# Retention and gated FFN on one core: x of pair 1 copied out by two engines and multiplied in chunks of 128 tokens, one v load and a few steps at other places

## The chip, the core and the metric

One core of a Trainium2 chip runs the whole program in one launch. TensorE (PE) multiplies, VectorE (DVE) and ScalarE (ACT) read its results out of PSUM, GpSimd (POOL) adds and multiplies in SBUF and issues the converting loads, SyncE (SP) issues stores and DMA transposes. The metric is device time in microseconds (us); lower is better.

## The reference, cut to what matters

```
B, H, S, D = 4, 8, 768, 64
gamma = 1.0 - 2.0 ** (-5.0 - np.arange(H))
for t in range(S):
    state = gamma * state + outer(k[:, :, t], v[:, :, t])
    y[:, :, t] = (q[:, :, t] @ state) / sqrt(D)
x = y.transpose(0, 2, 1, 3).reshape(3072, 512)
gate = sigmoid(x @ w_gate)             # 512 x 1536
out = (gate * (x @ w_val)) @ w_out     # 1536 x 512
```

A decaying linear attention over 4 batches and 8 heads gives x of 3072 tokens by 512; a sigmoid-gated FFN with 1536 hidden columns follows. Inputs and output are fp32 in HBM; the kernel multiplies in bf16.

## The kernel before, in words

The recurrence is done by chunks of 128 tokens. A *tile* t (0 to 5) is one chunk of each of the four batches: 512 columns of the FFN. It is made of two *pairs*: pair P holds chunk P//2 of batches 0 and 1 (P even) or 2 and 3 (P odd), and c (0, 1) is the batch in it. For each pair and c: q and k are transposed to `qkT` (on PE, lines 193 to 210, or by DMA, line 219), `scores` (line 238) multiplies them, `mask` (line 243, DVE) applies the decay and gives `st` in bf16, `inter` (line 253) multiplies q with the carried state, `intra` (line 258) adds `st` times v, and `y_out` (lines 261 to 273) writes 128 columns of `xT`, the FFN's input. `state` (line 280, PE), `state_sum` (lines 287 and 290, DVE) and `state_out` (line 295, ACT) carry the state on. The FFN of a tile goes by blocks of 128 hidden columns: gate and value products on PE (lines 305 and 309, four along d_model), the sigmoid on ACT (line 329), gate times value on DVE (line 332). Tile 1 takes blocks two by two over half of its columns (`up_half`, `half_sigmoid`, `half_finish`). Later tiles use a seven-product scheme, whose sums of weights and of hidden columns are prepared on POOL and DVE (lines 361, 456 and 474).

`mm` (line 303) issues a product either whole (128 weight columns, line 305) or as two halves of 64 weight columns (line 309); a step whose name is written in capitals is issued whole.

Two things set the order. First, straight code up to line 622: loads, the attention of pairs 0 and 1, and the first FFN block of tile 0, which starts on columns 0 to 255 (pair 0) and goes on with columns 256 to 511 (pair 1). Then `ORDER`, one string a tile, is read from left to right, and each word issues one step: `mk10` is mask number 10 (pair 2, c 1, half 0), `in5` and `ia5` are `inter` and `intra` of pair 2, c 1, `yo5` is its `y_out`, `vm11` the value block 11 and `mu11` its finish, `sg` a sigmoid, `tp7` and `te7` the PE transpose of q of pair 3 and its copy on ACT, `ag2` and `ag6` gate blocks of tile 1 over its first 256 columns, `sc6` scores of pair 3, `sm5` the state products of pair 5, `zs` and `zo` its sum and copy, `dp`, `dc`, `da`, `ds` products, copies, adds and stores of the second FFN product, `hs` and `hg` sums of hidden columns on DVE and POOL, `wp` and `aw` sums of weights on POOL. A `+` or `-` behind a word takes it for the next or the previous tile. Every engine works through its own part of this list in order, and waits are on counters of the other engines.

PSUM has eight banks; one holds the state products and seven are handed out by a table, `PLACES["ff"]`, in order of use. So a step that takes a bank waits until the bank's last reader is done. `PLACES["st"]` does the same for the masked scores.

Loads of k, q and v that convert to bf16 go through POOL's queue (line 96). Pair 5 is the second half of tile 2's k, q and v. Eight counters serve these loads in turn: the ninth load's issue waits until the first has landed.

Of the kernel before, what the change touches and what calls it, by code (L numbers as in the profile page):

```python
# [17 lines left out]
def kernel(  # L18
# [14 lines left out]
    C = 128  # L33
# [23 lines left out]
        "gs": "01234501234503215034203502345102354130524301453201540321453034035412031524",  # L57
        "maskd": "01",
        "ff": (
            "012345601230465102346523105246310542631405314056321602341562034163412045632516523560132601562306"  # L60
            "251062562015020324512065630653102651604250142343624015405400652016203541034046326504510416035253"
            "245132541351025162405034123406520512341234160532120605410531324"
        ),
        "qkT": "010231230123",
        "kt": "0101100101",
        "st": "012345670123456702134675120346752104637563245710",
        "xT": "010101",
        "hT": "010101",
        "scr": "010101101001101010010101010101",
# [12 lines left out]
    def held_in(P, n):  # L82
        held = {"k": kn, "q": qn, "v": vn}[n]
        t, j = divmod(P, 2)
        if (n, t) not in lands:
            lands[n, t] = place(ld, [C, 4 * H, D], BF16, tag=n, name=n + "n")
        for i in range(2):
            held[2 * t + i] = lands[n, t][:, i * 2 * H:(i + 1) * 2 * H, :]
        return held[P]

    def load(P, *what, pairs=1):
        t, j = divmod(P, 2)
        for n in what:
            held_in(P, n)
            x = {"k": k, "q": q, "v": v}[n]
            nc.gpsimd.dma_start(out=lands[n, t][:, j * 2 * H:(j + pairs) * 2 * H, :],  # L96
                                in_=x[2 * j:2 * (j + pairs), :, t * C:(t + 1) * C, :].rearrange("b h s d -> s (b h) d"))
# [85 lines left out]
    qkT, kt, sc, st, y, zz, za, xT = {}, {}, {}, {}, {}, {}, {}, {}  # L183

    def bank(shape, dt=F32):
        return place(pf, shape, dt, tag="ff", name="ff", padded_shape=[128, 2 * NP, C] if dt == BF16 else None)
# [62 lines left out]
    def inter(P, c):  # L249
        y[P, c] = bank([128, NP, C])  # L250
        if P > 1:
            for p in range(NP):
                mm(y[P, c][:, p, :], zbd[P % 2][:, c, p, :], qkT[P][:, 1, c, p, :], start=(p == 0), stop=False)

    def intra(P, c):
        for p in range(NP):
            for i in range(2):
                nc.tensor.matmul(y[P, c][i * D:(i + 1) * D, p, :], heads(vn[P], c)[:, 2 * p + i, :],  # L258
                                 st[P, c, i][:, p, :], start=(P < 2 and p == 0), stop=True, skip_group_check=True)

    def y_out(P, c, eng="a"):
        t = P // 2
        if t not in xT:
            xT[t] = place(at, [128, NP, 512], BF16, tag="xT", name="xT")
        col = (P % 2 * 2 + c) * C
        o = xT[t][:, :, col:col + C]
        if eng == "av":
            nc.scalar.copy(o[:, :NP // 2], y[P, c][:, :NP // 2])
            nc.vector.tensor_copy(o[:, NP // 2:], y[P, c][:, NP // 2:])
        elif t == 0:  # L270
            (nc.scalar.copy if eng == "a" else nc.vector.tensor_copy)(o, y[P, c])  # L271
        else:
            nc.vector.tensor_tensor(o, y[P, c], taby0, op=ALU.mult)  # L273
# [29 lines left out]
    def mm(o, left, right, **kw):  # L303
        if whole[0]:
            nc.tensor.matmul(o, left, right, skip_group_check=True, **kw)  # L305
            return
        for i in range(2):
            half = slice(i * D, (i + 1) * D)
            nc.tensor.matmul(o[half], left[:, half], right, skip_group_check=True, **kw)  # L309
# [8 lines left out]
    def up(t, n1, which, lo=0, hi=512):  # L318
        if (t, n1, which) not in us:
            us[t, n1, which] = bank([128, 512])  # L320
        w = (wg, wv)[which]
        for kk in range(KT):
            mm(us[t, n1, which][:, lo:hi], w[:, kk, n1 * 128:(n1 + 1) * 128], xT[t][:, kk, lo:hi],
               start=(kk == 0), stop=(kk == KT - 1))

    def up_sigmoid(t, n1, lo=0, hi=512):
        if (t, n1) not in gated:
            gated[t, n1] = place(ffn, [128, 512], F32, tag="gs", name="gs")
        nc.scalar.activation(gated[t, n1][:, lo:hi], us[t, n1, 0][:, lo:hi], AX.Sigmoid)
# [231 lines left out]
    def hold(P):  # L561
        nc.gpsimd.tensor_copy(kept[:, :2], qkT[P][:, :, 1, NP - 1, C - 1])

    def hold_for_sums(t):
        nc.gpsimd.tensor_copy(kept[:, 2:3], hs[t][:, 2, NFF // 2 - 1, :1])


    def y_step(P, c, eng="a"):
        inter(P, c)
        intra(P, c)  # L570
        y_out(P, c, eng)
# [26 lines left out]
    nc.scalar.preload_act_table(AX.Sigmoid)  # L598
    up(0, 0, 0, 0, 256)
    up(0, 0, 1, 0, 256)  # L600
    y_step(1, 0, "v")
    y_step(1, 1, "a")
    up_sigmoid(0, 0, 0, 256)
    up_finish(0, 0, 0, 256)
    us.clear()
    gated.pop((0, 0))
    for which in range(2):
        up(0, 0, which, 256, 512)
    up_sigmoid(0, 0, 256, 512)
    up_finish(0, 0, 256, 512)  # L610
    for s in range(3, NFF // 2 - 1):
# [7 lines left out]
    for s in range(4):  # L619
        load_out(s)  # L620
    load(4, "k", "q", "v")
    load(5, "k", "q", "v")

    STEPS = {
        "gm": lambda t, n: up(t, n, 0),
# [38 lines left out]
        "lk": lambda t, P: load(P, "k", pairs=2),  # L664
        "lq": lambda t, P: load(P, "q", pairs=2),
        "lv": lambda t, P: load(P, "v", pairs=2),
        "ho": lambda t, P: hold(P),
        "hi": lambda t, n: hold_for_sums(t),
        "xk": lambda t, P: xbar(P, 0),
# [128 lines left out]
```

## Time and profile before

| what | value |
|---|---|
| time before, median of 3 runs | 224.1 us (224.1, 226.42, 215.31) |
| the profiled execution's own time | 215.9 us |
| its span, first to last instruction | 214.2 us |
| clock granted to TensorE in it | 1.000 |
| PE busy | 204.6 us of the span, 96% |
| DVE, ACT, POOL busy | 189.2, 147.5, 139.5 us |
| HBM read, written | 28.31 MB, 6.29 MB |

Times in the profile count from the start of the span. In a timeline a row is: start, duration, engine, line, operation, output <- inputs, shape (partitions*weight columns for a PE row), count, and in brackets the idle time before it and what ended it. A PE row of several matmuls runs until the last result is out; the next row may begin before, since matmuls are pipelined. So the pace of a stream is read from start to start. "PEld" is the loading of weights.

### The profile page before, as it was taken

How to read it: one execution, taken by the hardware profiler on the slowest of the kernel's cores; microseconds unless marked ns; L12 is line 12 of the kernel's file. 1: busy time of each engine (PE TensorE's matmuls, PEld its weight loads, DVE VectorE, ACT ScalarE, POOL GpSimd, SP SyncE). 2: the span in 40 equal slices, each digit the busy share in tenths (PEclk: the TensorE clock that was granted, in tenths of full speed). 3: DMA queues.
4: the chain of work that ended last, by engine and by line, in shares of the span. 5: the costliest groups of instructions: out<-in, count | busy, mean ns of one | idle time of the engine just before them, and what ended most of it. 6: DMA issues, size and time to landing. Idle time of an engine off the chain costs nothing.

```text
span 214.2 us, 7187 instructions
## 1 busy us (share of the span) xinstructions
PE 204.6 (96%) x2938; PEld 177.3 (83%) x2938; DVE 189.2 (88%) x406; ACT 147.5 (69%) x396; POOL 139.5 (65%) x145
## 2 busy tenths in 40 slices
PE   6778999999999999999999999999999999999994
PEld 6555555778888998899988889998899988888883
DVE  6587979989999999979999899999999999968971
ACT  6384466543994389786869798787768969577731
POOL 8977784679999946699764279875618537024500
PEclk9999999999999999999999999999999999999999
DMA  9999999999995999969995129998121000023305
GB/s 125 143 170 194 195 173 165 183 199 159 159 132 33 98 156 143 204 126 157 170 227 115 49 99 163 159 105 127 49 101 52 3 0 3 0 50 70 75 25 183
DMA packets 103922, 25.38 MB, mean 118 GB/s; under 512 B 93904, under 2 KB 101072, under 8 KB 103888
## 3 DMA queue, kind: packets, MB, share of 16 engines
q0 software_dynamic: 81104, 13.90, 84.6%
q1 hardware_dynamic: 22640, 10.88, 28.6%
q8 instruction: 23, 0.38, 0.7%
q10 hardware_dynamic: 144, 0.13, 0.2%
q14 instruction: 11, 0.09, 0.1%
HBM read 28.31 MB, written 6.29 MB: 162 GB/s over the span
## 4 chain that ended last, share of the span: by engine, by line
PE 76%; DMA 14%; POOL 4%; DVE 3%; issue 1%; ACT 0%; ACTq 0%; DVEq 0%; POOLq 0%
PE ff L305 41%; PE ff L309 29%; DMA qn<-in_q_dram 6%; DMA wg<-in_moe_w_gate_dram 4%; DMA vn<-in_v_dram 4%; PE ff L238 2%; PE ff L258 2%; DVE scr L414 1%; POOL kn L96 1%; PE z L280 1%; DVE gs L435 1%; DVE xT L273 1%; POOL vn L96 1%; POOL qn L96 1%; POOL kn L104 1%
## 5 line engine op out<-in xcount | busy, mean ns | idle before, releaser
L420 POOL TENSOR_TENSOR hT<-gs,scr 128x512 bf16<-128x512 f32 x17 | 22.1, 1302 | 21.4 <-ACT gs L440 9.0
L430 ACT COPY gs<-ff 128x256 f32<-128x256 f32 x72 | 25.6, 377 | 11.1 <-PE ff L305 5.7
L409 ACT COPY scr<-ff 128x256 f32<-128x256 f32 x72 | 25.2, 375 | 6.5 <-PE ff L309 3.6
L414 DVE TENSOR_TENSOR scr<-scr,ff 128x512 f32<-128x512 f32 (+1 forms) x48 | 25.6, 547 | 3.5 <-ACT scr L409 1.3
L435 DVE TENSOR_TENSOR gs<-gs,ff 128x512 f32<-128x512 f32 (+1 forms) x48 | 25.8, 548 | 3.2 <-PE ff L305 2.0
L510 ACT COPY ob<-ff 128x256 f32<-128x256 f32 x48 | 17.7, 375 | 15.2 <-PE ff L305 8.9
L243 DVE TENSOR_TENSOR st<-ff,maskd 128x512 bf16<-128x512 f32 x40 | 25.7, 682 | 0.9 <-PE ff L238 0.9
L440 ACT ACTIVATE gs<-gs 128x512 f32<-128x512 f32 (+1 forms) x48 | 24.7, 530 | 2.3 <-DVE gs L435 2.2
L309 PE MATMUL ff<-xT,wg 128*64 128x256 bf16 (+1 forms) x268 | 24.2, 308 | 0.0
L309 PEld LDWEIGHTS <-wg 128*64 128x64 bf16 x356 | 19.4, 110 | 4.1 <-issue 0.4
L423 POOL TENSOR_TENSOR hT<-gs,scr 128x256 bf16<-128x256 f32 x16 | 11.9, 747 | 15.9 <-ACT gs L440 12.0
L309 PE MATMUL ff<-xT,wv 128*64 128x256 bf16 (+1 forms) x220 | 21.5, 311 | 0.0
L305 PEld LDWEIGHTS <-hT 128*128 128x128 bf16 x198 | 19.2, 98 | 2.7 <-issue 0.2
L305 PE MATMUL ff<-wo,hT 128*128 128x256 bf16 x156 | 21.0, 273 | 0.0
L309 PEld LDWEIGHTS <-wv 128*64 128x64 bf16 x312 | 17.2, 110 | 4.2 <-issue 0.3
L305 PEld LDWEIGHTS <-wv 128*128 128x128 bf16 x184 | 17.7, 98 | 2.4
L305 PEld LDWEIGHTS <-wg 128*128 128x128 bf16 x162 | 15.7, 98 | 3.8 <-issue 1.1
L309 PE MATMUL ff<-xs,ws 128*64 128x256 bf16 x208 | 18.7, 273 | 0.0
L305 PE MATMUL ff<-xT,wv 128*128 128x256 bf16 (+1 forms) x134 | 18.5, 276 | 0.0
L231 ACT ACTIVATE kt<-kn,tabk 128x128 bf16<-128x128 bf16 x48 | 18.3, 405 | 0.1
L309 PEld LDWEIGHTS <-ws 128*64 128x64 bf16 x308 | 17.2, 110 | 0.3
L305 PE MATMUL ff<-xT,wg 128*128 128x256 bf16 x110 | 15.4, 272 | 1.6 <-ACT xT L271 1.6
(118 smaller groups left out, 526.8 us busy)
## 6 DMA issues: line engine op xcount, KB each, us to landing
out_dram<-ob SPq DMA_DIRECT2D x18, 256.0 KB, 3.3
vn<-in_v_dram POOLq DMA_DIRECT2D x6, 256.0 KB, 12.4
wo<-in_moe_w_out_dram POOLq DMA_DIRECT2D x4, 384.0 KB, 14.2
kn<-in_k_dram POOLq DMA_DIRECT2D x3, 512.0 KB, 7.8
qn<-in_q_dram POOLq DMA_DIRECT2D x3, 512.0 KB, 10.0
vn<-in_v_dram POOLq DMA_DIRECT2D x3, 512.0 KB, 11.6
out_dram<-ob SPq DMA_DIRECT2D x11, 128.0 KB, 2.2
kn<-in_k_dram POOLq DMA_DIRECT2D x5, 256.0 KB, 13.4
```

The costliest lines, as they stand in the source:

```text
L231: nc.scalar.activation(to[:, :, h, :], x[:, :, h, :], AX.Copy, scale=tabk[:, 0, h:h + 1])
L243: nc.vector.tensor_tensor(st[P, c, i], sc[P, c][i], (mask0 if P < 2 else maskd)[:, i], op=ALU.mult)
L305: nc.tensor.matmul(o, left, right, skip_group_check=True, **kw)
L309: nc.tensor.matmul(o[half], left[:, half], right, skip_group_check=True, **kw)
L409: nc.scalar.copy(vals[t, g][:, {1: 0, 5: 2, 3: 1}[n]], m[False][:, 256:] if n == 1 else m[True][:, :256])
L414: nc.vector.tensor_tensor(o, o, x, op=ALU.add)
L420: eng.tensor_tensor(h[:, 2 * g], s, vals[t, g][:, 0:2].rearrange("p two n -> p (two n)"), op=ALU.mult)
L423: eng.tensor_tensor(h[:, 2 * g + 1, 256:], s[:, 256:], vals[t, g][:, 2], op=ALU.mult)
L430: nc.scalar.copy(o, pairs[t, g, 0][x][:, :256] if x else pairs[t, g, 0][x][:, 256:])
L435: nc.vector.tensor_tensor(o, o, pairs[t, g, 0][False][:, cols], op=ALU.add)
L440: nc.scalar.activation(o, x, AX.Sigmoid)
L510: nc.scalar.copy(o, fast[t, i][x][:, :256] if x else fast[t, i][x][:, 256:])
```

## The change

1. **Prelude, pair 1.** `y_step(1, 0)` and `y_step(1, 1)` each split their copy into `xT`: ACT takes the first half of the rows p (lines 268), DVE the second (line 269). Before, DVE did the whole of c 0 and ACT the whole of c 1. The first FFN block on columns 256 to 511, a gate and a value product of four matmuls of 256 columns each, becomes gate and value on columns 256 to 383 and then on 384 to 511: 16 matmuls of 128 columns in place of 8.
2. **v of pair 5** is loaded by a new step `lw5` behind `hg6-` in tile 1's string, not with k and q of pair 5 at line 622.
3. **Tile 1's string, start.** All four masks of pair 2 come first, then `in5 in4 ia5 ia4 yo5 yo4`, and then `vm11`, `mu10` and `mu11`; `in4` is issued in two halves; the gate block `ag2` stands ahead of `tp7`.
4. **Small moves.** Farther on in tile 1, `dc11-` and `dc15-` (ACT) stand ahead of two scalings of k, and `hs7-` (DVE) ahead of `bm4`. In tile 2, `sm6` stands behind `gp57`, not ahead of `vp47`.
5. `PLACES["ff"]` and `PLACES["st"]` are numbered anew from there on.

```
-    y_step(1, 0, "v")
-    y_step(1, 1, "a")
+    y_step(1, 0, "av")
+    y_step(1, 1, "av")
...
-    for which in range(2):
-        up(0, 0, which, 256, 512)
+    for lo in (256, 384):
+        for which in range(2):
+            up(0, 0, which, lo, lo + C)
...
-    load(5, "k", "q", "v")
+    load(5, "k", "q")
...
+        "lw": lambda t, P: load(P, "v"),
...
-        "zo0- wp1 gm7- wp4 gm8- tp5- vm8- mu4- sg7- sg8- te5- gm11- sc4- sc5- gm10- sg10- mu6- mu8- mk10- mk8-  "
-        "mk11- wp8 vm10- mu10- wp2 in5 ia5 vm11- IN4 mk9- ia4 yo5 tp6 yo4 aw13 sg11- te6 mu11- tp7 te7 dd5 dd15  "
+        "zo0- wp1 gm7- wp4 gm8- tp5- vm8- mu4- sg7- sg8- te5- gm11- sc4- sc5- gm10- sg10- mu6- mu8- mk10- mk11-  "
+        "mk8- mk9- wp8 vm10- wp2 in5 in4 ia5 ia4 yo5 yo4 vm11- mu10- tp6 aw13 sg11- te6 mu11- ag2 tp7 te7 dd5  "
```

Three places of the built program show what moves. In these rows a number before the `x` of a shape is partitions, and what an instruction waits for stands in brackets: `PE_49` and `Activation_49` are the counters of PE and ACT, `DMASW1_49` one of the loads' counters.

DVE in the prelude, around the copies of x of pair 1, before:

```order
L243 TENSOR_TENSOR st<-ff,mask_123 128x512 [waits PE_49] x4
L271 CAST xT<-ff 128x4x128 [waits PE_49]
L332 TENSOR_TENSOR hT<-gs,ff 128x256 [waits Activation_49]
L332 TENSOR_TENSOR hT<-gs,ff 128x256 [waits PE_49,Activation_49]
L361 TENSOR_TENSOR ws<-wv 128x256 [waits DMASW1_49]
```

and the same engine and place now:

```order
L243 TENSOR_TENSOR st<-ff,mask_123 128x512 [waits PE_49] x4
L269 CAST xT<-ff 128x2x128 [waits Activation_49] x2
L332 TENSOR_TENSOR hT<-gs,ff 128x256 [waits Activation_49]
L332 TENSOR_TENSOR hT<-gs,ff 128x256 [waits PE_49,Activation_49]
L361 TENSOR_TENSOR ws<-wv 128x256 [waits DMASW1_49]
```

One copy of 512 elements has become two of 256, and these wait for ACT, where the one waited for PE.

DVE at the start of tile 1's string, as one piece of the difference (L243 the masks of pair 2, L332 the finishes `mu`, L273 `yo5` and `yo4`):

```order
 L332 TENSOR_TENSOR hT<-gs,ff 128x512 x3
-L243 TENSOR_TENSOR st<-ff,maskd 128x512 x3
-L332 TENSOR_TENSOR hT<-gs,ff 128x512
-L243 TENSOR_TENSOR st<-ff,maskd 128x512
-L273 TENSOR_TENSOR xT<-ff,taby_138 128x4x128 x2
-L332 TENSOR_TENSOR hT<-gs,ff 128x512
+L243 TENSOR_TENSOR st<-ff,maskd 128x512 x4
+L273 TENSOR_TENSOR xT<-ff,taby_138 128x4x128 x2
+L332 TENSOR_TENSOR hT<-gs,ff 128x512 x2
 L361 TENSOR_TENSOR ws<-ws,wg 128x256
```

The fourth mask and both outputs of x have moved ahead of a finish (`mu10`).

POOL, as two pieces of the difference: where the loads of tile 2 end and the sums of weights begin, and 14 instructions later, behind `hg6` (L474):

```order
 L96 DMA kn<-in_k_dram 128x16x64
 L96 DMA qn<-in_q_dram 128x16x64
-L96 DMA vn<-in_v_dram 128x16x64
 L361 TENSOR_TENSOR ws<-wv 128x256
 L456 TENSOR_TENSOR wt<-wo 128x512
```

Here the issue is gone; the second piece, behind the sum `hg6`, has it:

```order
 L361 TENSOR_TENSOR wg<-wg 128x2x128
 L474 TENSOR_TENSOR hT<-hT 128x2x256
+L96 DMA vn<-in_v_dram 128x16x64
 L456 TENSOR_TENSOR wt<-wo,scr 128x512
 L456 TENSOR_TENSOR scr<-wo 128x512
```

The load of v has moved past 14 sums that POOL makes.

More of the change, by code (lines that the diff above doesn't have):

```diff
@@ L59 @@
         "ff": (
-            "012345601230465102346523105246310542631405314056321602341562034163412045632516523560132601562306"
-            "251062562015020324512065630653102651604250142343624015405400652016203541034046326504510416035253"
-            "245132541351025162405034123406520512341234160532120605410531324"
+            "012345601230465102346523105246310542631405314056321632045631205430541256301643610634201432461036"
+            "142361461324313015421364603640231642635143251050615324534533641326130452305356016435423526304140"
+            "154201452042314261534305210536413421052105263401213634523402015"
         ),
@@ L65 @@
         "kt": "0101100101",
-        "st": "012345670123456702134675120346752104637563245710",
+        "st": "012345670123456701234675210346751204637563145720",
         "xT": "010101",
```

12 rows, old and new, of the table ORDER are left out of this document.

## Prediction

> **What bounds the kernel now.** I read the page first: the slices of the span and the chain that ended last. The granted clock is 1.000 (table above), so no part of the sum hangs on it.
>
> ```profile
> PE   6778999999999999999999999999999999999994
> ...
> PE 76%; DMA 14%; POOL 4%; DVE 3%; issue 1%; ACT 0%; ACTq 0%; DVEq 0%; POOLq 0%
> ```
>
> From the fifth of 40 slices on (21 us) PE is at nine tenths or more, and three quarters of the chain are PE. The change removes no matmul, so it can only win or lose in the few places where PE waits. Then I read the timeline of each engine at the places that the diff touches. The end of the prelude on PE (intra of pair 1, gate, value, the first block of the string):
>
> ```profile
> 16.30 0.64 PE L258 MATMUL ff<-st,vn 128*64 128x128 bf16 x16
> 17.61 0.60 PE L305 MATMUL ff<-xT,wg 128*128 128x256 bf16 x4 [0.68 <-ACT xT L271]
> 18.05 0.60 PE L305 MATMUL ff<-xT,wv 128*128 128x256 bf16 x4
> ```
>
> PE stands for 0.68 us there, for the two copies of x, which run side by side on two engines:
>
> ```profile
> 16.75 0.69 DVE L271 CAST xT<-ff 128x512 bf16<-128x512 f32 x1 [0.98 <-PE ff L258]
> 16.98 0.59 ACT L271 CAST xT<-ff 128x512 bf16<-128x512 f32 x1 [0.61 <-PE ff L258]
> ```
>
> The second place is the start of tile 1's string: `ia5`, `vm11`, `IN4`, `ia4`, `tp6`, `tp7`, `ag2` with `ag6`, `sc6` with `sc7`:
>
> ```profile
> 38.16 0.52 PE L258 MATMUL ff<-st,vn 128*64 128x128 bf16 x8
> 38.49 1.05 PE L309 MATMUL ff<-xT,wv 128*64 128x512 bf16 x8
> 39.48 0.40 PE L305 MATMUL ff<-qkT,zbd 128*128 128x128 bf16 x4
> 39.81 0.41 PE L258 MATMUL ff<-st,vn 128*64 128x128 bf16 x8
> 40.05 0.61 PE L200 MATMUL ff<-ident,kn 128*64 128x128 bf16 x16
> 41.02 0.64 PE L200 MATMUL ff<-ident,qn 128*64 128x128 bf16 x16 [0.36 <-DMA qn<-in_q_dram]
> 41.49 1.91 PE L309 MATMUL ff<-xT,wg 128*64 128x256 bf16 x32
> 43.34 0.62 PE L238 MATMUL ff<-qkT 64*128 64x128 bf16 x16
> ```
>
> PE waits 0.36 us for q of pair 3. That is the last time a load holds it.
>
> **The change, part by part.**
>
> *Copies of x in halves, chunks of 128.* The built program says that the DVE half of a copy waits for ACT, not for PE: both halves lie in one PSUM bank, and they go one after the other. The trace has no such half copy. The nearest rows are ACT copies and DVE adds over 256 elements out of PSUM:
>
> ```profile
> L409 ACT COPY scr<-ff 128x256 f32<-128x256 f32 x72 | 25.2, 375 | 6.5 <-PE ff L309 3.6
> ```
> ```profile
> 104.55 0.41 DVE L516 TENSOR_TENSOR ob<-ob,ff 128x256 f32<-128x256 f32 x1
> ```
>
> With 0.38 and 0.41: ACT copies its half of c 0 from 16.75 to 17.13 and that of c 1 to 17.51; DVE follows from 17.13 to 17.54 and to 17.95. Before, c 0 was done at 16.75 + 0.69 = 17.44 and c 1 at 16.98 + 0.59 = 17.57. So x of pair 1 is complete 0.4 us later, not earlier. What makes up for it is that the products begin sooner. For the pace of 128-column matmuls with 128 weight columns I take the eight of `in8` and `in9`, up to the start of the next row:
>
> ```profile
> 65.51 0.61 PE L305 MATMUL ff<-qkT,zbd 128*128 128x128 bf16 x8
> 65.96 1.04 PE L305 MATMUL ff<-xT,wv 128*128 128x256 bf16 x8
> ```
>
> That is 0.45 / 8 = 0.056 us each; the 256-column ones take (18.05 - 17.61) / 4 = 0.11. So 16 small ones cost 0.90 against 0.88, nothing. The first two need ACT's half alone and run at 17.2. The other six of chunk 1 begin at 17.6, behind DVE's half, and end at 17.94; two of chunk 2 follow, the last six begin at 18.05 and end at 18.39. Before, the stream ended at 17.61 + 0.88 = 18.49. Gain 0.1 us. The bounds: if the halves ran side by side, c 0 would be done at 17.16, c 1 at 17.57, the stream would start at 17.2 and end at 18.1, a gain of 0.4. If the small matmuls went at the pace of their weight loads, they would lose:
>
> ```profile
> L305 PEld LDWEIGHTS <-wg 128*128 128x128 bf16 x162 | 15.7, 98 | 3.8 <-issue 1.1
> ```
>
> At 0.098 us each, chunk 1 ends at 18.19 and chunk 2 at 18.97, a loss of 0.5. The row of `in8` is nearest in kind (same line, same shape), so I keep the gain of 0.1. ACT's sigmoid and DVE's finish of these columns come about 0.1 us later than before; no matmul of the next microsecond reads them.
>
> The Trainium skill, "TensorE: Matmul & The Clock Gate", section "Back-to-back issue gap", speaks against the chunks: it states about 81 ns for a sustained pair of weight load and matmul of 128 columns. By it the second chunk would end at 18.77, an estimate, 0.3 us later than now, which lies between my two paces; the row of `in8` stands against it.
>
> *Masks, `in4`, `ag2`.* On DVE the same stretch reads:
>
> ```profile
> 36.36 1.89 DVE L243 TENSOR_TENSOR st<-ff,maskd 128x512 bf16<-128x512 f32 x3
> 38.22 0.69 DVE L332 TENSOR_TENSOR hT<-gs,ff 128x512 bf16<-128x512 f32 x1
> 38.82 0.68 DVE L243 TENSOR_TENSOR st<-ff,maskd 128x512 bf16<-128x512 f32 x1
> 39.42 0.68 DVE L273 TENSOR_TENSOR xT<-ff,taby 128x512 bf16<-128x512 f32 x1
> 40.26 0.69 DVE L273 TENSOR_TENSOR xT<-ff,taby 128x512 bf16<-128x512 f32 x1 [0.16 <-PE ff L258]
> ```
>
> A mask takes 1.89 / 3 = 0.63, so four end at 36.36 + 2.52 = 38.88 (before, the last at 39.50). PE now does `in5`, `in4`, `ia5` and could do `ia4` at 38.6, but waits for the fourth mask until 38.9: a new wait of 0.3. `vm11` starts 0.24 later (as `tp6` after `ia4` before) at 39.15, `tp6` 0.99 after that at 40.14, `ag2` at 40.14 + 0.47 = 40.61. It needs both outputs of x: DVE makes them from 38.88 to 39.5 and from 39.5 to 40.2, so 0.4 in hand. `ag2` takes (43.34 - 41.49) / 2 = 0.92, `tp7` starts at 41.53 and no longer waits for q, there since 41.0. But the copy of its result, `te7`, is now late:
>
> ```profile
> 40.71 2.01 ACT L210 COPY qkT<-ff 128x1024 bf16<-128x1024 bf16 x2 [2.34 <-PE ff L200]
> ```
>
> A copy takes 1.0. Before, `te7` was done at 42.72, 0.6 ahead of `sc6`, with both gate blocks between. Now only `ag6` is between: `tp7` has its last result at 41.53 + 0.64 = 42.17, `te7` ends at 43.17, `ag6` at 42.9, so PE waits 0.27 and `sc6` starts at 43.2. Gain 0.14, where 0.4 is the upper bound (no wait at `sc6`); as lower bound I take a loss of 0.3, if the new wait at `ia4` came on top. `in4` in halves costs eight matmuls in place of four that run two at a time, nothing. `mu10` and `mu11` come later on DVE; the banks that they free are taken next by `sc6`, 2 us on.
>
> *v of pair 5.* POOL loses one issue and the wait ahead of it, and makes the issue behind `hg6` (60.77):
>
> ```profile
> 46.41 1.14 POOL L96 DMA_DIRECT2D vn<-in_v_dram  x1 [0.59 <-DMA wo<-in_moe_w_out_dram]
> ```
> ```profile
> 60.77 1.34 POOL L474 TENSOR_TENSOR hT<-hT 128x512 bf16<-128x512 bf16 x1
> ```
>
> So the 14 sums between go up to 1.73 us sooner; nobody on PE waits for them, so that earns nothing. The issue falls between 60.4 and 62.1. Its first reader is `sm5` on PE, with everything of PE behind it:
>
> ```profile
> 69.58 0.44 PE L280 MATMUL z<-vn,kt 128*64 128x64 bf16 x16
> ```
>
> How long a load of 256 KB takes there no row shows. The nearest above it is the median of the v loads, taken while the queue was full; the nearest below, the first load of pair 6, twice the size, in an empty queue (landing time behind it):
>
> ```profile
> vn<-in_v_dram POOLq DMA_DIRECT2D x6, 256.0 KB, 12.4
> ```
> ```profile
> 68.74 1.72 POOL L96 DMA_DIRECT2D kn<-in_k_dram  x1
> ```
> ```profile
> DMA to landing us min/median/max: 7.8/7.8/7.8
> ```
>
> With 7.8 it lands at 68.2 to 69.9, at worst 0.3 late; with 12.4 at 72.8 to 74.5, up to 4.9 late. The traffic says which is nearer:
>
> ```profile
> GB/s 125 143 170 194 195 173 165 183 199 159 159 132 33 98 156 143 204 126 157 170 227 115 49 99 163 159 105 127 49 101 52 3 0 3 0 50 70 75 25 183
> ```
>
> The slice from 64 to 70 us moves 33 GB/s, so the queue runs empty, and the load is half of pair 6's. I take less than 7.8, no wait, cost 0. It shares the engines with the two transposes of pair 5 on SP; what they move is the same in sum, and `sc10`, which needs them, comes only just ahead of `sm5`:
>
> ```profile
> 57.44 2.13 SPq L219 DMA_TRANSPOSE qkT<-kn  x1
> 61.44 1.57 SPq L219 DMA_TRANSPOSE qkT<-qn  x1
> ```
>
> *Small moves and banks.* `sm6` goes behind `gp57`, into a place where PE waits for DVE:
>
> ```profile
> 109.02 0.61 DVE scr L414
> 109.62 0.04 issue
> 109.67 0.41 PE ff L309 x4
> ```
>
> DVE sets 109.67 there, so 0, within 0.25 either way. `dc11`, `dc15` and `hs7` keep their engines' sums of work: 0, within 0.2. With the banks numbered anew a few steps wait for another reader; those I could match with rows had finished in time before. 0, and up to 0.5 if one is late.
>
> **The sum** is made against the profiled execution's own 215.9 us (span 214.2 and 1.7 around it): 215.9 - 0.1 - 0.14 = 215.7. This lies beside the lowest of the three runs, 215.31, and 8.4 below their median, 224.1. The profile shows nothing that makes 224, so the sum cannot speak of it. Own range of this case, from gains of 0.4 + 0.4 + 0.25 + 0.2 to losses of 0.5 + 0.3 + 0.25 + 0.2 + 0.5: 214.6 to 217.7.
>
> **Rivals.** (1) *It does what the words say*: halves side by side and no wait at `sc6`: 0.4 + 0.4 off, 215.1. For it: two copies did run side by side before. Against: DVE's wait for ACT, and one ACT copy between `tp7` and `sc6`. (2) *The small matmuls go at weight-load pace*: 0.5 lost, 0.14 gained, 216.3. The row of `in8` is against it. (3) *Slower: v of pair 5 lands late.* With 12.4 us, 4.9 - 0.24 more: 220.6. It decides where issue to landing passes 7.5 to 9.2 us. For it: 12.4 is what half of the loads of this size took or passed. Against: the empty slice. (4) *The level of the runs*: the unchanged program gave 215.31 and 226.42. If the changed one's median falls at 224 to 226, or at 215.7 beside a median of 224.1, a difference is read that no step of the change explains.
>
> **How the numbers follow.** My case 0.55, (1) 0.10, (2) 0.07, (3) 0.06, (4) 0.22, of which 0.14 reads as faster and 0.08 as slower. A measurement of this kernel tells about 2% (4.3 us) from no change. Only the upper half of (3) passes that, 0.03. So faster 0.14, same 0.75, slower 0.11. The time is that of the likeliest case, 215.7. The range runs from 214.4, a little under its own lower end, to 226.0: it takes in (3) and nearly all of the spread of the unchanged program.
>
> **What would show it.** Right: after it, a DVE half of x that starts when ACT's ends, and gate and value on pair 1 done within 0.2 us of before; no wait for q at `tp7`, but one of about 0.3 at `ia4` and at `sc6`; v of pair 5 issued at 60 to 62 and no wait at `sm5`. Wrong: `sm5` waiting for a load, an `ACT` and a `DVE` half that overlap, or a new PE wait in tiles 1 to 3 for a bank's reader.

## The result and the profile after

| kernel | median | runs |
|---|---|---|
| before | 216.06 us | 14 (215.13 to 226.42) |
| after | 217.11 us | 14 (216.15 to 224.7) |

The ratio is 1.0043, 95% interval 1.0024 to 1.0061: the change costs 0.9 us, where 0.2 us of gain was forecast. The size was missed and so was the sign; the difference is under 2%. The ratios here and below leave out executions that took over 1.5% more than the fastest of their kernel (in one later run two of 735 and 536 us, unexplained), and the one first profiled for after, at 220.07 us, is among them, so the rows of after below are, where nothing else is said, from a further execution of the same kernel at 216.66 us, span 215.0, clock 1.000.

The page of the kernel after, the slices and the chain that ended last:

```profile
PE   6779999999999999999999999999999999999994
...
PE 82%; DVE 12%; ACT 3%; issue 1%; ACTq 0%; DVEq 0%
```

PE still bounds everything from the fifth slice on. DVE now has 12% of the chain and not 3%; but it has 10% too in the run below that loses nothing (all but the move of v), so this share does not show where the time goes. First the end of the prelude, in the timelines of PE, ACT and DVE:

```profile
16.04 0.64 PE L258 MATMUL ff<-st,vn 128*64 128x128 bf16 x16
16.49 0.65 ACT L268 CAST xT<-ff 128x256 bf16<-128x256 f32 x2 [0.17 <-PE ff L258]
16.90 0.76 DVE L269 CAST xT<-ff 128x256 bf16<-128x256 f32 x2 [1.22 <-ACT xT L268]
16.92 0.27 PE L305 MATMUL ff<-xT,wg 128*128 128x128 bf16 x2 [0.24 <-ACT xT L268]
17.71 0.39 PE L305 MATMUL ff<-xT,wg 128*128 128x128 bf16 x4
17.93 0.39 PE L305 MATMUL ff<-xT,wv 128*128 128x128 bf16 x4
18.25 0.84 PE L309 MATMUL ff<-xT,wg 128*64 128x512 bf16 x6
```

DVE's half starts behind ACT's first half, the first two small matmuls run on ACT's half alone, and four of them take 17.93 - 17.71 = 0.22 us, 0.055 each. From the start of `intra` to the first block of the string it was 18.58 - 16.30 = 2.28 us; it is 18.25 - 16.04 = 2.21 (`intra` is the first row, the block the last).

The start of tile 1's string on PE, and POOL around the moved load:

```profile
38.22 0.92 PE L258 MATMUL ff<-st,vn 128*64 128x128 bf16 x16
38.96 1.05 PE L309 MATMUL ff<-xT,wv 128*64 128x512 bf16 x8
41.14 0.64 PE L200 MATMUL ff<-ident,qn 128*64 128x128 bf16 x16
42.88 0.62 PE L238 MATMUL ff<-qkT 64*128 64x128 bf16 x16 [0.23 <-ACT qkT L210]
```
```profile
45.56 0.68 POOL L361 TENSOR_TENSOR ws<-wv 128x256 bf16<-128x256 bf16 x1
...
54.69 1.15 POOL L456 TENSOR_TENSOR scr<-wo 128x512 f32<-128x512 bf16 x1 [1.80 <-ACT wo L460]
...
61.61 1.19 POOL L96 DMA_DIRECT2D vn<-in_v_dram  x1
62.81 1.35 POOL L456 TENSOR_TENSOR wt<-wo,scr 128x512 bf16<-128x512 bf16 x1
```

The two `intra` now take 0.74 together, where the rows of before give 0.33 and 0.24, so PE waits about 0.17 there; `tp7` waits for nothing, `sc6` 0.23. POOL begins its sums 2.0 us sooner, and gives that back at 52.9, where it waits 1.80 us for a copy on ACT. At 61.6 it makes the issue, and its next sum starts at 62.81; in the kernel before that was

```profile
62.06 1.21 POOL L456 TENSOR_TENSOR wt<-wo,scr 128x512 bf16<-128x512 bf16 x1
```

Now the place where the time goes. In each fence one row of POOL, DVE and PE; first before, then after:

```profile
75.70 1.17 POOL L371 TENSOR_TENSOR xs<-xT 128x512 bf16<-128x512 bf16 x1
...
76.94 0.42 DVE L474 TENSOR_TENSOR hs<-hT 128x512 bf16<-128x512 bf16 x1
...
79.08 0.39 PE L309 MATMUL ff<-xT,ws 128*64 128x256 bf16 x4
```
```profile
76.44 1.17 POOL L371 TENSOR_TENSOR xs<-xT 128x512 bf16<-128x512 bf16 x1
...
76.82 1.08 DVE L474 TENSOR_TENSOR hs<-hT 128x512 bf16<-128x512 bf16 x1
...
79.42 0.41 PE L309 MATMUL ff<-xT,ws 128*64 128x256 bf16 x4 [0.29 <-DVE ws L361]
```

Before, POOL's difference of x (`xg1`) ended at 76.87, just ahead of DVE's sum `hs8` at 76.94. After, it starts 0.74 us later, `hs8` starts into it and takes 1.08 us in place of 0.42, ending 0.29 us behind POOL. Eight sums stand in a row on DVE there; `dd3`, the fifth, comes late, and the products `gp03` on PE wait for it.

The table shows how far PE is behind (+) or ahead (-) of the profiled execution of before, in us, at the first matmul of one `scores` or `state` step each (its start in the one trace less that in the other). The head gives the time in before. The first column is start-up, which differs from execution to execution.

| kernel | 23.8 | 43.3 | 69.0 | 77.5 | 88.7 | 156.5 |
|---|---|---|---|---|---|---|
| after (216.66) | -0.33 | -0.46 | -0.11 | -0.11 | +0.56 | +0.75 |
| all but the move of v | -0.08 | -0.41 | -0.11 | -0.11 | -0.11 | -0.11 |
| prelude alone | -0.27 | -0.70 | -0.70 | -0.70 | -0.69 | -0.76 |
| order alone | -0.18 | -0.51 | -0.23 | -0.23 | -0.22 | -0.29 |
| before, `dd7` early | -0.19 | -0.56 | -0.57 | -0.57 | -0.57 | -0.56 |
| after, `dd7` early, second profile | -0.05 | -0.15 | +0.07 | +0.07 | +0.75 | +0.84 |
| v in POOL's idle time | -0.08 | -0.41 | -0.23 | -0.23 | -0.24 | -0.26 |
| spare sum in place of v | +0.52 | +0.20 | +0.59 | +0.59 | +1.23 | +1.21 |

Two losses stand out: 0.2 to 0.4 us from 43 to 69 in the kernels with the new order, and 0.64 to 0.68 us from 77.5 to 88.7 in those with something more on POOL behind `hg6`. The second makes most of the difference of 0.86 at the end between the first two rows, and of 216.66 - 215.80 = 0.86 between these executions.

### The profile page after: what moved, and what is told of

Read it like the earlier page. It is cut to its first block, busy times and chain, and to the rows that moved or that the text cites. A ratio compares the mean times of both kernels' runs of the same rounds, so it can differ in the third digit from the quotient of the medians.

```text
span 218.4 us, 7212 instructions
## 1 busy us (share of the span) xinstructions
PE 205.7 (94%) x2950; PEld 178.1 (82%) x2950; DVE 189.0 (87%) x407; ACT 147.4 (67%) x397; POOL 139.5 (64%) x145
## 4 chain that ended last, share of the span: by engine, by line
PE 78%; DVE 11%; DMA 4%; POOL 3%; issue 1%; ACT 1%; ACTq 0%; DVEq 0%; POOLq 0%
PE ff L305 39%; PE ff L309 34%; DMA vn<-in_v_dram 4%; PE ff L238 2%; PE ff L258 2%; DVE st L243 2%; DVE ws L361 2%; DVE hT L349 1%; DVE hs L474 1%; PE z L280 1%; DVE hT L332 1%; DVE scr L414 1%; DVE kt L228 1%; DVE xT L273 1%; POOL qn L96 1%
## 5 line engine op out<-in xcount | busy, mean ns | idle before, releaser
L243 DVE TENSOR_TENSOR st<-ff,maskd 128x512 bf16<-128x512 f32 x40 | 25.6, 680 | 0.6 <-PE ff L238 0.6
L305 PE MATMUL ff<-wo,hT 128*128 128x256 bf16 x156 | 21.5, 276 | 0.0
L305 PEld LDWEIGHTS <-wv 128*128 128x128 bf16 x188 | 18.2, 100 | 2.7
L305 PE MATMUL ff<-xT,wv 128*128 128x256 bf16 (+2 forms) x138 | 19.5, 281 | 0.0
L305 PEld LDWEIGHTS <-hs 128*128 128x128 bf16 x150 | 14.6, 98 | 3.7 <-DVE hs L474 1.9
```

Of the source, the lines that this page charges most:

```text
L243: nc.vector.tensor_tensor(st[P, c, i], sc[P, c][i], (mask0 if P < 2 else maskd)[:, i], op=ALU.mult)
```

## The experiments

Ratios are to the kernel before on the same chip. The edits are made to after unless the text says before.

**Which part costs.** The change was cut in pieces. The move of v alone, put into before:

```
-    load(5, "k", "q", "v")
+    load(5, "k", "q")
+        "lw": lambda t, P: load(P, "v"),
-am6 zo6 hg6- BV0
+am6 zo6 hg6- lw5 BV0
```

> Before with the one edit that v of pair 5 is loaded by the new step behind hg6. Theory (POOL's sums of weights start 1.7 us sooner and come to lie beside DVE's sums, which then take until POOL's instruction ends): 1.004 to 1.008 of before, with a DVE sum of about 1.2 us in place of 0.28 near 45 us and a PE wait of some 0.5 to 1 us behind it. Rival A (the new order of masks, finishes and banks costs the time): 1.000. Rival B (the late load itself holds the state product of pair 5): slower by as much, but with PE waiting for a load near 70 us.

1.0079 (1.0034 to 1.0124). The opposite, after with v loaded at line 622 again:

> After with v of pair 5 loaded at its old place; chunks, halves, order and banks as in after. Theory: 0.4 to 0.5 us off, 0.997 to 0.999 of before, since the waits at tp7 and in the prelude are shorter and POOL's sums lie where they lay. Rival A (order and banks): 1.004, as after. Rival B (late load): like the theory, 0.997 to 1.000.

0.9998 (0.9976 to 1.0019). So the move of v is the price. The rest was split: before with lines 601, 602 and the chunks of 128 (prelude alone), and after without these and without the move (order alone).

> Before with only the copies of x of pair 1 in halves and the chunks of 128. Theory and rivals A and B alike: PE reaches the first block of the string 0.1 to 0.15 us sooner, which is lost in the wait for q at tp7: 0.999 to 1.001 of before. If the prelude were the cause, 1.004.

0.9976 (0.995 to 1.0001).

> After without the prelude's part and with v of pair 5 at its old place: the new order of steps and the new banks alone. Theory: 0.1 to 0.4 us off, 0.998 to 1.000 of before. Rival A (order and banks are the cause): 1.004.

0.999 (0.9967 to 1.0013). After itself once more:

> After unchanged, beside the others on one chip and for a second profile. Theory: 1.002 to 1.006 of before, with dd7 near 45 us over 1 us long and PE behind it waiting. Rival C: the same time, with dd7 at about 0.3 us and a delay that begins near 62 us.

1.0069 (1.0034 to 1.0105).

**First theory: `dd7`.** POOL's sums now run at 45 us beside DVE's sum `dd7`. In the profile of the v move alone it took

```profile
45.31 4.44 DVE L361 TENSOR_TENSOR ws<-wg,ws 128x256 bf16<-128x256 bf16 x1
```

in place of 0.28: POOL went through 45.59, 46.23, 47.34 and 48.45 without a gap, and `dd7` ended in the first gap (49.60 to 49.79), at 49.75. So `dd7` was taken out of POOL's way, in after and, as a control, in before:

```
-sc6 mk12 ... wp5 dd7 ag0
+sc6 dd7 mk12 ... wp5 ag0
```

> After with one step of DVE moved: the sum of weights dd7, which stood behind the masks of pair 3 and stretched to 1.3 us in the profile of after and 4.4 us in that of e1, now stands ahead of them, where DVE idles and POOL still issues loads. Theory (that sum, caught beside POOL's sums, is what costs): 0.997 to 0.999 of before, like e2, with every sum of this line near 45 us at 0.28 us. Rival C (what costs is the later issue itself, 1.2 us on POOL among its sums near 62 us and what it delays): 1.003 to 1.005, as after.

1.0064 (1.0036 to 1.0091).

> Before with dd7 moved in the same way, a control: the sum stood clear of POOL there already. Theory and rival C alike: 0.999 to 1.001 of before.

1.0005 (0.999 to 1.002). The theory fell: `dd7` takes 0.29 us in the first, and the loss stays, at 77 to 88 us. `dd7` can cost, but it isn't what makes the ratio of after.

**Early gap or late issue.** v of pair 5 loaded twice, at line 622 and at `lw5`:

```
+    load(5, "k", "q", "v")
```

> After with v of pair 5 loaded at its old place and once more behind hg6 (the second load brings the same values). POOL's sums start where they started before, and the later issue stays. Theory: 0.998 to 1.000 of before. Rival C: 1.003 to 1.005, as after.

1.0136 (1.0107 to 1.0165). The late issue costs also where nothing is earlier. The second load waits 1.93 us on POOL for the first to land, so wait and issue take 3.1 us of POOL, more than the issue alone in after, and PE ends 2.4 us behind before. `sc11` waits 1.10 us there for a sigmoid on ACT, which stands behind a copy that waits 4.3 us for POOL's sum: a second way by which POOL's lateness reaches PE.

**POOL's time or the load.** In the first kernel v stays behind the early gap but is issued in POOL's idle time (`dd7` early too); in the second v is at its old place, and a sum that nobody reads stands where `lw5` was:

```
-wp5 dd7 ... hg6- lw5 BV0
+lw5 wp5 ... hg6- BV0
```
```
+        nc.gpsimd.tensor_tensor(spare, maskd[:, 0], mask0[:, 0], op=ALU.add)
-am6 zo6 hg6- lw5 BV0
+am6 zo6 hg6- du0 BV0
```

> The kernel after, with the sum dd7 ahead of mk12 as in the run with dd7 moved, and v of pair 5 issued not behind hg6 (61.3 us) but ahead of POOL's first sum of wp5, where POOL stood idle for 2.44 us (51.94 to 54.38). Theory A, POOL's time: what costs is the 1.19 us of the issue at 61.3, which puts all that POOL does up to its next idle time (77 us) later, so that its x difference comes beside the sum hs8 on DVE (1.09 us where 0.42 was) and the product behind it waits. In the idle time the issue moves nothing: POOL's sums of 54 to 77 stand as without the moved load (0.2 to 0.5 us ahead of the kernel before), hs8 takes 0.42, TensorE stays 0.2 to 0.5 us ahead, ratio 0.997 to 1.002 (215.2 to 216.0 us). Theory B, the load itself: it still leaves 5 us later than in the kernel before and its transfer still falls among the others; then the cost stays, ratio 1.004 to 1.009. Theory C, the early start of POOL's sums (45.0 in place of 47.6 us) costs by itself: then too the cost stays, ratio 1.004 or more.

1.0003 (0.9986 to 1.002).

> The kernel of the run with v in POOL's idle time once more (dd7 ahead of mk12, v of pair 5 ahead of wp5), for an undisturbed profile and a second interval. By the theory that POOL's time is the price: POOL's sums from 54 us on stand as in the kernel with all but the move of v, hs8 takes 0.42 us, TensorE 0.1 us ahead to 0.6 us ahead of the kernel before from 43 to 157 us; ratio 0.997 to 1.002. By the rivals (the load's transfer, the early start of POOL's sums): TensorE loses 0.3 us or more somewhere between 47 and 92 us, ratio 1.003 or more.

1.0002 (0.9981 to 1.0022). `hs8` takes 0.42, and PE loses 0.03 us from 69 to 157 us.

> The kernel with all but the move of v (v of pair 5 loaded at its old place), with dd7 ahead of mk12, and behind hg6, where the load was put, one more POOL sum of two 128x512 tables into a tile that nobody reads: about 1.2 us of POOL (the sums of that size take 1.15 to 1.34 us), no load. Theory A (POOL's time): POOL's later work moves by 1.2 us, its x difference starts at 76.5 us, hs8 on DVE takes 0.9 us or more in place of 0.42, TensorE loses 0.4 to 0.7 us between 77 and 88 us; ratio 1.002 to 1.007 (215.9 to 217.0 us). Theory B (the load itself) and theory C (the early start, absent here): nothing is lost, ratio 0.997 to 1.001.

1.0059 (1.0025 to 1.0092). The spare sum on POOL, then the three rows of the place:

```profile
62.25 1.32 POOL L563 TENSOR_TENSOR spare<-maskd,mask 128x512 bf16<-128x512 f32 x1
```
```profile
77.14 1.17 POOL L371 TENSOR_TENSOR xs<-xT 128x512 bf16<-128x512 bf16 x1
```
```profile
77.53 1.06 DVE L474 TENSOR_TENSOR hs<-hT 128x512 bf16<-128x512 bf16 x1
```
```profile
80.10 0.41 PE L309 MATMUL ff<-xT,ws 128*64 128x256 bf16 x4 [0.27 <-DVE ws L361]
```

With no load there at all the same sum is caught and the same product waits. POOL's time behind `hg6` is the price, not the load.

**`dd7` by itself.** v in POOL's idle time, `dd7` left where it is in after:

> The kernel after with v of pair 5 issued in POOL's idle time ahead of wp5, and dd7 left where the change has it. It tells what dd7 beside POOL's early sums costs by itself. Theory A with dd7 as a second cost: dd7 takes 1.27 us or more, TensorE is 0.5 to 0.8 us later from 48 us on than in the run with dd7 moved as well; ratio 1.001 to 1.005, and 1.01 or more if dd7 is held for 4.4 us as it was with the load's move alone. If dd7 is free in most executions: as that run, 0.997 to 1.002.

1.0029 (0.9991 to 1.0066): not settled. In its profile (222.02 us) `dd7` took 3.86 us and PE waited 2.7 us.

**The best parts together**: the prelude in before, with `dd7` early.

> The first part of the change alone (both x conversions split over two engines, the products of pair 1 by 128 tokens), and dd7 ahead of mk12; v of pair 5, the masks, in4 and sm6 as in the kernel before. The first part alone gave 0.9976 (0.995 to 1.0001), dd7 moved alone 1.0005. Theory: they add up, TensorE 0.5 to 0.8 us ahead throughout; 215.2 to 215.6 us, ratio 0.995 to 0.999. Rival: the gain of the first part was chance, ratio 0.999 to 1.001.

0.9994 (0.9975 to 1.0012). The gain of the prelude alone, 0.9976, was not seen again; no version beats the kernel before by what can be told.

**Is `hs8` the only way?** `hs8` ahead of POOL's difference, with the load and with the spare sum (`dd7` early in both):

```
-am8 da06- zo10 hs8
+am8 hs8 da06- zo10
```

> The kernel after with dd7 ahead of mk12, as in that run, and on DVE the sum hs8 ahead of da06 instead of behind it, so that it starts at 75.9 us, ahead of POOL's late x difference (76.16 to 77.32 us). v of pair 5 stays behind hg6. Theory: the path by which POOL's lateness costs is hs8 caught beside that difference (1.09 us, and then dd3 late and the product of gp03 waits 0.3 us, 0.45 us of TensorE lost). hs8 takes 0.42 us, hs9 starts by 77.4 us and takes at most 0.9 us, TensorE loses less than 0.2 us between 77 and 88 us in the profile; ratio 1.002 to 1.006, below the 1.0064 of the run with dd7 moved alone by 0.001 to 0.004. Rival: the cost comes by other waits (the late weight sums and their copies on ACT, which hold the sigmoid behind them): TensorE's loss stays 0.4 us or more, ratio 1.005 to 1.009.

1.0048 (1.0024 to 1.0072).

> The kernel with the spare POOL sum behind hg6 (no moved load, dd7 ahead of mk12) with hs8 ahead of da06 on DVE. Spare sum alone: hs8 1.06 us, ratio 1.0059. Theory (hs8 beside the x difference is the path): hs8 0.42 us, TensorE's loss at 79 us (0.45 us) falls below 0.2 us; ratio 1.001 to 1.005. Rival (other waits): ratio 1.005 to 1.008 and the loss at 79 us stays.

1.0056 (1.0031 to 1.0082). In both profiles `hs8` takes 0.42, and the loss from 77.5 to 88.7 falls from 0.67 to 0.24; yet the ratios stay about where they were, and tell neither forecast from the other. The two profiled executions, 216.05 and 216.08 us, lie below the medians of their kernels (217.17 and 217.03), so they need not show what makes these. Then one more profile of three kernels, after (the rows above), after with `dd7` early (in the table), and with `hs8` early too:

> The kernel after itself, one more profiled execution: both earlier ones were disturbed (220.07 and 220.18 us, where the median is 217.1). Theory: in an execution near the median the loss of 1 to 1.5 us of TensorE against the kernel with all but the move of v lies where DVE's sums of two SBUF tiles run beside POOL's sums: dd7 at 44.7 us (1.27 us in place of 0.28), the sums of the hidden tile at 60 to 65 us, hs8 at 77 us (1.1 in place of 0.42); 216.5 to 217.5 us. Rival: it lies in a wait for the load of v (the state product at 69 us starts late), or is spread over the rest of the program.

> The kernel after with dd7 ahead of mk12, one more profiled execution: the first one was among the fastest of its kernel (216.26 us, median 216.73). Theory: 216.3 to 217.3 us; TensorE loses 0.6 us or more between 77 and 88 us again, by hs8 (0.9 us or more) beside POOL's x difference, and up to 0.5 us at 60 to 70 us by DVE's sums there. Rival: the loss lies elsewhere from one execution to the next.

> The kernel after with dd7 ahead of mk12 and hs8 ahead of da06, one more profiled execution: the first one was the fastest of its kernel (216.05 us, median of the undisturbed ones 217.0). Theory: what is left of the price lies at 60 to 70 us, where DVE's sums of the hidden tile run beside POOL's late sums and the scores wait for a bank (0.4 to 1.0 us lost there); 216.5 to 217.3 us. Rival: TensorE is not later than in the first profile anywhere, and the execution takes 216.0 to 216.3 us.

216.66, 216.76 and 216.97 us. In the first two it is `hs8` again: 1.08 and 1.10 us. In the third the loss is not at 60 to 70 us, where it was expected: PE is 0.11 ahead of before at 88.7 and 1.14 behind at 92.6, by two other pairs of sums, DVE and then POOL:

```profile
89.46 0.93 DVE L423 TENSOR_TENSOR hT<-gs,scr 128x256 bf16<-128x256 f32 x1 [0.16 <-ACT gs L440]
...
90.91 0.78 DVE L361 TENSOR_TENSOR ws<-wg,ws 128x256 bf16<-128x256 bf16 x1
```
```profile
89.38 0.73 POOL L423 TENSOR_TENSOR hT<-gs,scr 128x256 bf16<-128x256 f32 x1 [1.90 <-DVE scr L414]
...
90.39 1.15 POOL L474 TENSOR_TENSOR hs<-hT,hs 128x512 bf16<-128x512 bf16 x1
```

In the earlier profile of the same kernel (216.05 us) DVE's sum of line 423 came 0.1 us ahead of POOL's and took 0.43. So `hs8` is the catch in the execution of after shown above, and when it is taken away another can come, decided by 0.1 us of which engine starts first.

**A third meeting, with the moved issue itself.** In the execution of after at 220.07 us `hs8` keeps its 0.42 us, and the loss lies earlier (first the same DVE sum, `dd17`, in before, then POOL, DVE and PE of that execution):

```profile
61.01 1.24 DVE L361 TENSOR_TENSOR ws<-ws,wg 128x256 bf16<-128x256 bf16 x1
```
```profile
61.92 1.19 POOL L96 DMA_DIRECT2D vn<-in_v_dram  x1
62.18 2.36 DVE L361 TENSOR_TENSOR ws<-ws,wg 128x256 bf16<-128x256 bf16 x1
...
64.46 1.37 DVE L474 TENSOR_TENSOR hs<-hT,hs 128x512 bf16<-128x512 bf16 x1
65.89 0.61 PE L305 MATMUL ff<-wo,hs 128*128 128x256 bf16 x4 [1.63 <-DVE hs L474]
```

`dd17` starts inside the moved issue, runs on through POOL's next sum (63.12 to 64.30), and PE waits 1.63 us for `hs7` behind it; at 69.0 PE is 4.22 us behind before. In an execution of after at 220.18 and in that of the v move alone (222.86) `dd17` takes 2.36 us too, and in no profiled kernel without the issue behind `hg6` does it take more than 1.25; in five other executions with it, it takes 1.24. What decides is again small: `hs11`, ahead of it on DVE, started 0.04 us behind `hg6` here and 0.07 us ahead of it in the execution of 216.66. So the move can cost 4 us in an execution, not only the 0.9 us of the ratio. How often it does is open; the kernel before took 224.1 and 226.42 us without it.

## Why the prediction was wrong

*The step that failed* is v of pair 5. It said of the sums made sooner "that earns nothing", which held, and of the load "I take less than 7.8, no wait, cost 0", which held for the load: it landed in 5.5 us, at 67.1, 2.3 us ahead of `sm5`. What the step left out is the issue as work of POOL. At its old place POOL waited for memory anyway, and the sooner start ends in a wait of 1.80 us for ACT. At the new place 1.19 us go into a stretch in which POOL has no idle time until 77 us. All that POOL does there stands 0.7 to 0.9 us later than before, and 1.1 us later at the x difference than with all but the move (76.44 for 75.33), and DVE's sum `hs8` runs into it. That was sized at 0 and measured 0.67 us on PE at this place; by the ratio of after (1.0043) against that of all but the move (0.9998), about 1 us. That POOL's time is the cause is shown by the spare sum and by v in idle time; that `hs8` is the way to PE holds for the profiles shown, while the ratios of 1.0048 and 1.0056 with `hs8` early leave open which meetings make the rest.

*Small moves* failed as well. "0, within 0.2" for `hs7` ahead of `bm4`: `hs7` now starts 0.12 us into the moved issue and takes 1.42 us in place of 0.78 (DVE; before, then after), and with the order alone it takes 1.38, beside a sum of POOL:

```profile
62.77 0.78 DVE L474 TENSOR_TENSOR hs<-hT,hs 128x512 bf16<-128x512 bf16 x1
```
```profile
61.73 1.42 DVE L474 TENSOR_TENSOR hs<-hT,hs 128x512 bf16<-128x512 bf16 x1
```

The finishes behind it are late for the second `scores` of pair 4. PE loses 0.28 us there with the order alone, nothing with the prelude alone or in before with `dd7` early. Of the 0.35 us between 43 and 69 in after, 0.18 lie there; the other 0.17 are lost at 47 to 48 us, where `intra` of pair 3 waits for a mask behind `dd7` (0.63 us in place of 0.28). This is read from traces; `hs7` was not moved back by itself.

*Masks, `in4`, `ag2`*: the mechanism was right, with waits of 0.17 and 0.23 for 0.3 and 0.27. `sc6` came 0.46 - 0.33 = 0.13 sooner than in the profile of before, as forecast (0.14). But the wait for q that it takes away was one of before's one profile: in before with `dd7` early and in the prelude alone `tp7` waits for nothing, and PE gains 0.37 and 0.43 between 23.8 and 43.3 without the new order. Against such executions the new order earns nothing, and agreement on 0.13 is luck.

*Prelude*: forecast 0.1, measured 0.07 in the trace, at the pace of the row of `in8` (0.055 for 0.056), not at that of the weight loads. (The estimate of 18.77 in that part should read 18.73.) `sm6` and banks: with all but the move of v nothing is lost from 69 to 157 us, so 0 was right. Of the 0.19 that after loses between 88.7 and 156.5, 0.13 come at 109 us, where DVE sets PE's pace and the sum of line 423 took 0.65 us beside POOL in place of 0.49; this too is only read from the trace.

*Rivals*: (1) and (2) did not come: the halves of a copy went one after the other, and the small matmuls did not go at the pace of weight loads. (3) had the right part of the change and the wrong reason, as `sm5` never waited. (4) was right in that the median of 224.1 from three runs did not last. That 217.11 lies inside the range is luck: its own range of 214.6 to 217.7 reaches so far only by losses that did not come (chunks at weight-load pace, a bank that is late), and the rest was opened for the spread of the runs.

The clue was in the profile of before. One line of sums on DVE, two tiles of SBUF in and no PSUM, with its least, median and longest duration in ns:

```profile
L361 DVE TENSOR_TENSOR ws<-ws,wg x5: 281/291/1241, 22.3 to 61.0; 128x256 bf16<-128x256 bf16 x5
```

The longest starts at 61.01 us, inside POOL's `hg6` (60.77 to 62.11), and ends 0.15 us behind it. Equal shapes that take 281 or 1241 ns point to something shared with another engine, and a move on POOL shifts which of them pay.

## What to carry to other kernels

A load's issue is work of the engine that issues it. Before moving it, find where that engine next stands idle: everything up to there moves by its length, and each piece of it can meet a sum of another engine. Put it into idle time, as here at 52.6 us, where the same load cost nothing that the runs can tell (1.0003 and 1.0002). And before a step is called free, look whether operations of one shape have very different longest durations.

## What the hardware showed

A DVE sum of two SBUF tiles that starts while POOL makes a sum runs until 0.15 us (line 361) to 0.3 us (line 474) behind POOL's end: `dd17` in before ended at 62.25 behind 62.11, `hs8` in after at 77.90 behind 77.61. The one that starts first keeps its time (0.42 for `hs8` at 76.21, ahead of POOL at 76.41, in the run with `hs8` early). The Trainium skill, "SBUF — State Buffer", section "Who interferes with whom", states the same: a DVE operation with two SBUF inputs and a GpSimd operation that reads SBUF take one port pair, and the order of issue decides who blocks. DVE operations with an input from PSUM, such as line 349, kept their time (0.68).

The start of POOL's sums does not settle everything here. `dd7` of 4.44 us started at 45.31, ahead of four sums of POOL that followed each other but inside an issue of POOL (44.44 to 45.58), and stayed held until POOL's first gap. `dd17` in before came free behind one sum, though POOL's next had begun. And a sum that starts inside an issue can also keep its time: line 371 in before took 0.43 us at 74.80, inside the issue of 73.96 to 75.68. What decides between these cases is open.

Long waits on PE can be followed by a lower granted clock. In the execution of after at 220.07 us, PE waited 1.63 us at 64 to 66 us, and the windows read (length, busy time and count of PE, PEld, DVE, ACT, POOL, then PEclk, the granted clock):

```profile
64.00:68.00 4.00, 2.16 (x27) 1.29 (x25) 4.00 (x6) 1.73 (x5) 4.00 (x5) 0.96 1.11 82
68.00:72.00 4.00, 4.00 (x28) 3.10 (x25) 2.70 (x5) 0.12 (x1) 3.98 (x6) 0.61 0.00 0
```

If the work goes with the clock, those 4 us at 0.61 do that of about 2.4, an estimate; between the `scores` steps that before does at 64.3 and 69.0 PE falls 2.08 us further behind before, the clock's share and other waits together. So a catch that lasts long can cost more than its length. It need not: in the execution of the v move alone a wait of 3.21 us was followed by 0.68 (52 to 56 us), one of 1.49 us at 69 to 71 us by 1.00 (72 to 76 us).
